# A new order for all engines' steps, and a fixed buffer for each batch

## The chip, the cores and the metric

The kernel runs on one core of a Trainium2 chip. The metric is the time of one execution on the device in microseconds; the runs of the kernel before took 207.67, 208.43 and 208.44 us, with a median of 208.43. The profile is of one execution, whose span (first to last instruction) is 205.4 us.

## The reference

`x` is 8 batches x 8 heads x 512 tokens x 64, `state` is 8 x 8 x 32 x 64. Attention goes both ways between tokens and states, and the joined rows (512 + 32 per batch, 8 heads x 64 = 512 wide, 4352 rows in all) go through a two-layer network with a PReLU:

```python
scores = x @ state^T / 8;  a = softmax(scores);   xread = a @ state
scores2 = state @ x^T / 8; a2 = softmax(scores2); sread = a2 @ x
rows = concat([xread, sread], axis=2)        # 544 rows of 512 per batch
h = rows @ w_in                              # 512 -> 2048
g = max(h, 0) + alpha * min(h, 0)
out = g @ w_out                              # 2048 -> 512, float32
```

## The kernel before

The whole program is one list of short tokens, `ORDER`. Each token names a step, with its batch, piece, PSUM bank and engine; a loop at the end of the kernel (line 830) calls the steps in this order. An engine runs its instructions in the order in which the tokens issue them, and a step starts when its inputs are there and the PSUM bank or buffer that it writes is free. There are eight PSUM banks, named in the tokens. So the order sets everything: which engine works on what, what queues behind a wait, and when transfers start.

The steps that matter here:

- Loads, all issued from GpSimd's queue: `lx0.g` (half the heads of batch 0, line 218), `lx.b` (x of a batch, line 201), `lst` (the states of batches 2 to 7, line 247), `wi.f` (a quarter of w_in, 512 of its columns, line 253), `wo.i` (a quarter of w_out, 512 of its rows, line 259). Stores `st.b.q` and halves `sv.b.q.h` go out on SP's queue, and so do the transposes by DMA, `xd` (line 327) and `tt` (line 541).
- States: `stt`, `sto`, `str`, `sro` transpose the states into `stT` (the copies out of PSUM: lines 300 and 317).
- Softmax for tokens: `sc` (scores on TensorE, line 362), `sb` (VectorE transposes them in blocks of 32), `smax`, `ssh` (GpSimd, line 482), `sexp` (ScalarE), `ssum`, `snorm` (GpSimd, line 496), `wb` (transposed back: the weights `aT`). Batch 0 goes by `sd`, `hm`, `hs`, `he` instead. Softmax for states: `tm`, `tms`, `te` (ScalarE, line 527), `tt`, `rd`, `rn`, `rt`, `rdo`.
- First layer without xread: since xread = a @ state, xread @ w_in is a @ (state @ w_in). `m.b.f` forms the product of a batch's states with a quarter of w_in (line 590, eight small matmuls side by side in two banks), `mo` copies its two halves out of PSUM (line 603, ScalarE or VectorE). `F.b.jc` (two matmuls, line 620; `f` is one of the two, line 641) gives one of 16 blocks of hidden rows from the weights and these products. For the state rows (b = 8) `F` goes the plain way with four matmuls (line 629). `N` is ScalarE's negative part (line 652), `G` VectorE's combination of both (line 656).
- Second layer: batch 0 in plain form, `S.b.q.i` (two matmuls of 512 columns, line 675) and `O`. All others by Strassen's scheme, with seven products instead of eight: `W` (sums of the blocks of w_out, GpSimd, line 745), `A.b.i.s.f` (sums of hidden rows, GpSimd or VectorE, line 765), `P.b.i.p.half` (four matmuls of 256 columns, line 793), `C` (copies out, line 805), `D` (added on, line 810). The products of one output lie in one bank one after the other, with a copy between: `P..1`, `C..1`, `P..6`, `C..2`, `P..7`, `C..3`, `P..4`, `C..4`.
- `Z.k.n` runs matmuls over zeros, n units of 128 columns.

Buffers that each batch needs anew (`xg`, `xT`, `ts`, `mx`, `r1`, `an`, `aT`, `e2`, `e2T`, `sn`) come from a pool that gives them out in turn, two to four of a kind. Sums of hidden rows have two buffers of a kind and half (the last number of an `A` token), output rows four.

Of the kernel before, what the change touches and what calls it, by code (L numbers as in the profile page):

```python
# [34 lines left out]
G.1.4 F.1.8.7 N.1.8.1 G.1.8 S.0.1.5 S.0.2.5 N.1.1.2 G.1.1 F.1.2.4 N.1.2.3 G.1.2 F.1.15.1 N.1.15.0
G.1.15 S.0.1.6 S.0.1.7 O.0.1.a.0 F.1.10.3 N.1.10.1 G.1.10 S.0.2.6 S.0.0.4 xd.2 sc.2.2.6.7 sb.2 tm.2
m.4.2.2.4 mo.4.2.a.0.12 smax.2 S.0.2.7 O.0.2.a.1 mo.4.2.a.1 S.0.3.0.1 F.1.9.3 N.1.9.2 G.1.9 tsum.1
F.1.11.2 N.1.11.3 G.1.11 W.0.0.p W.2.1.p W.0.1.p W.2.0.p W.3.1.p W.3.0.p A.1.0.3.0.p.0 A.1.1.3.0.p.1
tms.2 te.2.1 F.1.6.5 N.1.6.0 G.1.6 S.0.3.1 S.0.3.2 F.1.7.4 S.0.0.5 te.2.0 N.1.7.1 G.1.7 S.0.0.6
S.0.0.7 O.0.0.a.2 tt.0 tt.1 rd.0.3 rd.1.6 rn.1 A.1.1.1.0.v.0 A.1.0.3.1.v.0 m.2.3.7.2 mo.2.3.a.0.13  # L40
mo.2.3.a.1 xd.3 st.0.2 st.0.1 tt.2 S.0.3.3 F.1.13.5 ssh.p.2 sexp.2 N.1.13.2 m.3.1.0.4 mo.3.1.a.1.1
mo.3.1.a.0 A.1.1.2.0.p.0 rn.0 sc.3.2.6.7 tm.3 tms.3 lx.4 A.1.0.1.0.p.1 ssum.2 snorm.p.2 S.0.3.4
P.1.1.1.0.2 F.1.14.3 P.1.1.1.1 G.1.13 N.1.14.3 G.1.14 A.1.1.1.1.p.0 S.0.3.5 S.0.3.6 P.1.0.2.0.4
P.1.0.1.0.0 S.0.3.7 te.3.0 te.3.1 tt.3 sb.3 P.1.1.2.0.5 P.1.1.2.1 C.1.1.1.a.3 D.1.1.0 P.1.0.1.1
O.0.3.a.1 st.0.3 st.0.0 tsum.2 wb.2 m.2.2.3.1 mo.2.2.a.1.4 mo.2.2.a.0 m.3.2.6.7 mo.3.2.a.0.6 rd.2.5
lx.5 xd.4 A.1.1.2.1.p.0 P.1.0.2.1 mo.3.2.a.1 rt.0.1 rdo.0.a rn.2 smax.3 P.1.1.6.0 A.1.0.2.0.v.1
A.1.0.4.0.p.0 F.2.7.3 N.2.7.0 G.2.7 F.2.1.5 N.2.1.1 G.2.1 C.1.0.1.a.0 D.1.0.0 F.2.8.6 N.2.8.2 G.2.8
F.2.2.7 F.2.3.1 N.2.2.3 N.2.3.0 G.2.2 P.1.0.6.0 F.2.5.3 N.2.5.1 P.1.1.6.1 F.2.0.5 N.2.0.2 G.2.5
G.2.3 P.1.0.5.0.4 C.1.1.2.a F.2.11.6 N.2.11.3 G.2.11 G.2.0 A.1.0.1.1.p.1 P.1.0.5.1 F.2.9.7 P.1.1.7.0
F.2.10.3 N.2.10.1 xd.5 G.2.10 F.2.4.1 N.2.9.0 G.2.9 F.2.14.6 N.2.4.3 G.2.4 N.2.14.2 G.2.14  # L50
A.1.1.3.1.p.1 A.1.0.2.1.p.1 P.1.0.6.1 C.1.0.2.a P.1.1.7.1 ssh.p.3 sexp.3 ssum.3 P.1.1.5.0.5 F.2.13.3
rt.2.7 rdo.2.a P.1.0.7.0 C.1.1.3.a.1 P.1.0.7.1 C.1.0.3.a.2 D.1.0.1 F.2.12.1 N.2.12.1 F.2.6.6
P.1.1.5.1 G.2.12 N.2.6.0 F.2.15.7 N.2.15.3 A.1.0.4.1.p.0 G.2.6 G.2.15 N.2.13.2 G.2.13 P.1.0.4.0
P.1.0.4.1 A.2.0.1.0.p.1 C.1.0.4.a A.1.1.4.0.p.1 P.1.0.3.0 A.2.1.3.0.p.1 P.1.0.3.1 D.1.0.2 st.1.0
D.1.1.1 P.1.1.4.0 P.1.1.4.1 C.1.1.4.a st.1.3 tsum.3 rd.3.6 rn.3 sc.4.2.0.1 snorm.p.3 wb.3 m.3.3.7.3
m.4.1.4.2 mo.4.1.a.0.9 mo.3.3.a.1.0 mo.3.3.a.0 A.1.1.4.1.p.1 A.2.0.2.0.p.1 P.1.1.3.0 mo.4.1.a.1
A.2.1.1.0.v.0 A.2.0.4.0.v.0 P.2.0.1.0.6 P.2.0.1.1 P.2.0.2.0.4 C.2.0.1.a.0 F.3.5.3 N.3.5.1
A.2.0.1.1.v.1 A.2.0.2.1.p.1 F.3.1.7 N.3.1.0 tm.4 tms.4 P.2.0.6.0 P.2.0.2.1 D.2.0.0 G.3.5 F.3.3.2
# [804 lines left out]
```

## Time and profile before

| | |
|---|---|
| median of the runs | 208.43 us (207.67 to 208.44) |
| span of the profiled execution | 205.4 us; its time around the span isn't listed, the median is 3.03 us above the span |
| busy | TensorE 197.1 us (96%), VectorE 181.6 (88%), GpSimd 159.6 (78%), ScalarE 145.2 (71%) |
| granted TensorE clock | 1.00 by the profile, in all stretches |
| first S (second layer of batch 0) | starts at 25.12 us |
| TensorE's last matmul | ends at about 201.9 us |
| HBM | 17.31 MB read, 8.91 MB written |

Busy time is the union of an engine's instructions, and a matmul's end is modelled, so a busy TensorE need not run at its pace. In the views, a row of the timeline gives the start, the length, the engine, the line, the operation, and in brackets the idle time before it with what ended it; x4 means that four like instructions are merged in one row.

### The profile page before, as it was taken

The numbers are of one execution on the slowest core, as the hardware profiler recorded it, in microseconds if no ns is written. First come the engines' busy times: TensorE is split into PE (matmuls) and PEld (weight loads), VectorE is DVE, ScalarE is ACT, GpSimd is POOL, SyncE is SP. The second block draws the span as 40 slices with busy tenths as digits, with TensorE's granted clock in tenths as the row PEclk, the third lists the DMA queues.
The fourth block names the chain that finished last, engine by engine and source line by source line (L and its number), as shares of the span: only waits on it lengthen the run. The fifth ranks groups of instructions, "written<-read, shape, count | busy, mean of one in ns | idle before, by whom it ended". The sixth has DMA issues, their size and how long they took to land.

```text
span 205.4 us, 5181 instructions
## 1 busy us (share of the span) xinstructions
PE 197.1 (96%) x2023; PEld 131.4 (64%) x2023; DVE 181.6 (88%) x321; ACT 145.2 (71%) x319; POOL 159.6 (78%) x136
## 2 busy tenths in 40 slices
PE   7887999999999999999999999999999999999993
PEld 2542344445757766766557776776778777788882
DVE  4799999999999989999899999989999699995841
ACT  2599997889897679899898878869666476411120
POOL 7575489999989979998998899987997988502220
PEclk9999999999999999999999999999999999999999
DMA  5999999995999342749990135022000220031124
GB/s 81 195 203 209 204 206 197 185 232 54 163 163 178 66 153 58 100 103 158 194 163 3 53 123 135 3 105 102 0 0 3 111 93 3 2 131 62 69 102 156
DMA packets 39257, 23.22 MB, mean 113 GB/s; under 512 B 22320, under 2 KB 35008, under 8 KB 39232
## 3 DMA queue, kind: packets, MB, share of 16 engines
q0 software_dynamic: 12704, 8.59, 29.3%
q1 hardware_dynamic: 26496, 14.29, 28.4%
q8 instruction: 16, 0.26, 0.6%
q14 instruction: 9, 0.07, 0.2%
q10 hardware_dynamic: 32, 0.01, 0.0%
HBM read 17.31 MB, written 8.91 MB: 128 GB/s over the span
## 4 chain that ended last, share of the span: by engine, by line
PE 85%; DVE 5%; DMA 5%; POOL 1%; ACT 1%; issue 1%; ACTq 0%; POOLq 0%
PE ps L793 44%; PE ps L620 24%; PE ps L675 7%; DMA xg<-in_x_dram 5%; PE ps L629 3%; PE ps L590 3%; DVE gt_all L656 3%; PE ps L553 1%; ACT neg_all L652 1%; PE ps L362 1%; DVE m_all L603 1%; POOL xg L218 1%; DVE ts L466 1%; DVE nb L514 1%; DVE mx L476 1%
## 5 line engine op out<-in xcount | busy, mean ns | idle before, releaser
L656 DVE SCALAR_TENSOR_TENSOR gt_all<-neg_all,oma_sb,ps 128x512 f16<-128x512 f32 x128 | 89.3, 738 | 3.0 <-ACT neg_all L652 2.7
L652 ACT ACTIVATE neg_all<-ps 128x512 f32<-128x512 f32 (+1 forms) x144 | 77.4, 598 | 20.0 <-PE ps L620 14.4
L620 PE MATMUL ps<-aT,m_all 128*128 128x512 f16 x250 | 66.4, 379 | 0.3 <-DVE m_all L603 0.2
L765 POOL TENSOR_TENSOR hc_all<-gt_all 128x512 f16<-128x512 f16 x43 | 49.2, 1160 | 11.4 <-DVE osb_all L810 8.7
L793 PEld LDWEIGHTS <-hc_all 128*128 128x128 f16 x480 | 46.3, 98 | 14.3 <-issue 1.1
L793 PE MATMUL ps<-wc,hc_all 128*128 128x256 f16 x360 | 47.7, 273 | 0.0
L793 PEld LDWEIGHTS <-gt_all 128*128 128x128 f16 x336 | 32.6, 98 | 8.3 <-issue 0.5
L805 ACT COPY osb_all<-ps 128x256 f32<-128x256 f32 x51 | 19.1, 383 | 25.7 <-PE ps L793 22.2
L620 PEld LDWEIGHTS <-m_all 128*128 128x128 f16 x250 | 24.0, 98 | 18.0 <-issue 2.2
L603 ACT CAST m_all<-ps 128x512 f16<-128x512 f32 x58 | 31.6, 621 | 4.3 <-PE ps L590 4.3
L765 POOL TENSOR_TENSOR hc_all<-gt_all,hc_all 128x512 f16<-128x512 f16 x22 | 25.4, 1164 | 6.3 <-DVE hc_all L765 6.1
L793 PE MATMUL ps<-w_out_sb,gt_all 128*128 128x256 f16 x224 | 29.7, 273 | 0.0
L765 POOL TENSOR_TENSOR hc_all<-hc_all,gt_all 128x512 f16<-128x512 f16 x21 | 24.3, 1164 | 3.9 <-DVE hc_all L765 3.6
L810 DVE TENSOR_TENSOR osb_all<-osb_all,ps 128x256 f32<-128x256 f32 x45 | 18.0, 413 | 7.6 <-PE ps L793 4.7
L496 POOL TENSOR_TENSOR an<-ts,r 128x1024 f16<-128x1024 f32 (+1 forms) x9 | 15.5, 1725 | 6.2 <-DVE r L493 4.0
L482 POOL TENSOR_TENSOR ts<-ts,mx 128x1024 f32<-128x1024 f32 x7 | 13.4, 1918 | 5.4 <-DVE mx L476 5.4
L675 PE MATMUL ps<-w_out_sb,gt_all 128*128 128x512 f16 x64 | 16.6, 380 | 0.1
L793 PE MATMUL ps<-w_out_sb,hc_all 128*128 128x256 f16 x120 | 16.5, 273 | 0.0
L793 PE MATMUL ps<-wc,gt_all 128*128 128x256 f16 x112 | 14.7, 273 | 0.0
L590 PE MATMUL ps<-w_in_sb,stT 64*32 64x512 f16 x256 | 11.8, 383 | 1.9 <-DMA w_in_sb<-in_moe_w_in_dram 0.9
L527 ACT ACTIVATE e<-ps,nb 128x512 f16<-128x512 f32 x16 | 11.1, 705 | 0.1
L675 PEld LDWEIGHTS <-gt_all 128*128 128x128 f16 x64 | 5.9, 98 | 7.2 <-issue 1.2
(78 smaller groups left out, 204.6 us busy)
## 6 DMA issues: line engine op xcount, KB each, us to landing
out_dram<-osb_all SPq DMA_DIRECT2D x33, 256.0 KB, 2.6
xg<-in_x_dram POOLq DMA_DIRECT2D x7, 512.0 KB, 9.1
w_in_sb<-in_moe_w_in_dram POOLq DMA_DIRECT2D x4, 512.0 KB, 12.0
w_out_sb<-in_moe_w_out_dram POOLq DMA_DIRECT2D x4, 512.0 KB, 13.6
xg<-in_x_dram POOLq DMA_DIRECT2D x2, 256.0 KB, 4.5
out_dram<-osb_all SPq DMA_DIRECT2D x2, 128.0 KB, 2.4
gs_all<-in_state_dram POOLq DMA_DIRECT2D x1, 192.0 KB, 6.8
st<-in_state_dram SPq DMA_DIRECT2D x1, 128.0 KB, 2.4
```

The source lines that it names most:

```text
L482: engine(e).tensor_tensor(ts, ts, over_blocks(cols(softmax_tile("mx", b), j, S // N)), ALU.subtract)
L496: engine(e).tensor_tensor(blocks(cols(softmax_tile("an", b), j, S)), blocks(cols(softmax_tile("ts", b), j, S)), over_blocks(cols(softmax_t ...
L590: nc.tensor.matmul(banks[N * k : N * (k + 1), (k0, k1)[g], :], st_head(b, 2 * k + g)[64 * g : 64 * g + 64, :], w_in_sb[64 * g : 64 * g + 6 ...
L603: copier(e)(ms[b, f][:, g, :], banks[:, live["mp", b, f][g], :])
L620: nc.tensor.matmul(h.rearrange("p (r t) -> p r t", r=2), ms[b, f][:, g, 128 * j : 128 * (j + 1)], weights(b, g), start=(g == 0), stop=(g = ...
L652: nc.scalar.activation(neg, h, RELU, bias=0.0, scale=-1.0)
L656: nc.vector.scalar_tensor_tensor(gts[b, f][:, j, :], negs.pop((b, jc)), oma_sb[:, jc : jc + 1], hs.pop((b, jc)), ALU.mult, ALU.add,)
L675: nc.tensor.matmul(outs[b, q], hidden(b, jc, q), w_out_sb[:, jc, :], start=(jc == 0), stop=(jc == n_jc - 1),)
L765: engine(e).tensor_tensor(t, x, y, ALU.add if s == 1 else ALU.subtract)
L793: nc.tensor.matmul(outs[b, i, bank], rows, cols, start=(p in (1, 2, 5) and jc == 0), stop=(jc == n_jc // 2 - 1), skip_group_check=True,)
L805: copier(e)(rows_at(b, q, k)[:, 256 * half : 256 * (half + 1)], outs[b, i, "x"])
L810: nc.vector.tensor_tensor(to, to, outs[b, i, bank], ALU.add)
```

## The change: a new order, and homes

All tokens of `ORDER` stand in a new order, with other PSUM banks. The steps of the sum stay (210 P, 144 F with their N and G, 32 S, 120 A, 64 mo, all loads and stores). What differs in kind: zero matmuls 66 units instead of 73, in other places; 96 hidden sums on GpSimd and 24 on VectorE instead of 88 and 32; 59 `mo` copies on ScalarE and 5 on VectorE instead of 58 and 6; both copies of the later states (`sro`) on ScalarE instead of one on each engine; one `xo` more on ScalarE, and one `dd` less.

The start of the order, before and after:

```diff
-lx0.0 lx0.1 id ni.v wi.0 oma lst stc Z.7.32 stt.2 sto.a lx.1 wi.1 dd.0.0.v wi.2 Z.7.3 xt.0.0.0.6
...
-xo.0.0.1.a sd.0.1.6 hm.0.1 sc.0.2.1.2 tm.0 hs.0.0 he.0.0 ssum.0.0 wi.3 Z.3.2 hs.0.1 he.0.1 ssum.0.1
-m.1.0.7.4 mo.1.0.a.1.0 m.0.0.3.0 mo.0.0.a.1.1 tms.0 mo.0.0.a.0 str.0.5 sro.0.a str.1.6 sro.1.v
-mo.1.0.v.0 snorm.p.0.0 wb.0.0 snorm.p.0.1 wb.0.1 wo.0 wo.1 wo.2 te.0.1 te.0.0 Z.4.17 m.2.0.0.3
-mo.2.0.a.1.2 mo.2.0.a.0 Z.4.5 xt.1.1.0.5 xt.1.0.0.5 xo2.1.0.v xt.1.1.1.6 xt.1.0.1.6 xo2.1.1.v
...
+lx0.1 lx0.0 lst id wi.0 ni.v stc Z.7.32 stt.0 dd.0.0.v Z.7.7 xt.0.1.1.1 xt.0.0.1.2 dd.0.1.v xo.0.1.1.v oma
+xo.0.0.1.a lx.1 sto.a Z.7.11 xt.0.1.0.3 xt.0.0.0.4 xo.0.0.0.a xo.0.1.0.v sd.0.1.5 hm.0.1 str.1.6 sd.0.0.7
+sc.0.2.1.2 sro.1.a hm.0.0 hs.0.1 he.0.1 tm.0 Z.0.3 hs.0.0 he.0.0 ssum.0.1 ssum.0.0 str.0.0 sro.0.a Z.3.12
+m.0.0.3.4 m.4.0.6.5 m.2.0.7.0 wi.1 mo.0.0.v.1.0 tms.0 wo.0 wi.2 wo.1 te.0.0 te.0.1 wi.3 mo.0.0.a.0 m.1.0.1.2
+mo.2.0.a.0.1 snorm.p.0.1 m.3.0.4.3 snorm.p.0.0 wo.2 lx.2 wb.0.1 mo.4.0.v.0.2 wb.0.0 mo.1.0.a.0.3 xt.1.1.0.7
+xt.1.0.0.7 xo2.1.0.v mo.3.0.a.1.4 xt.1.1.1.6 xt.1.0.1.6 mo.1.0.v.1 xo2.1.1.v f.0.0.0.1 f.0.0.1 wo.3
+f.0.2.0.3 mo.3.0.a.0 mo.2.0.a.1 mo.4.0.a.1 N.0.0.0 F.0.3.4 f.0.1.0.7 f.0.1.1 N.0.3.1 G.0.0 m.0.1.0.5 N.0.1.2
...
```

The first S steps, and the end of the order:

```diff
-S.0.1.0.2 S.0.1.1 S.0.2.0.5 S.0.2.1 m.2.1.6.4 mo.2.1.v.0.10 sexp.1 ssum.1 snorm.p.1 N.0.6.1 G.0.6
...
-P.7.0.5.1 D.7.0.0 D.7.0.1 A.7.0.4.1.v.1 P.7.0.4.0 P.7.0.4.1 C.7.0.4.a st.7.1 P.7.1.7.0 P.7.1.7.1
-C.7.1.3.a.3 P.7.1.5.1 D.7.1.1 sv.7.3.1 P.7.0.3.0 P.7.0.3.1 D.7.0.2 st.7.0 A.7.1.4.0.p.0 P.7.1.3.0
-P.7.1.3.1 D.7.1.2 st.7.2 P.7.1.4.0 P.7.1.4.1 C.7.1.4.a sv.7.3.0
+m.2.1.0.5 mo.2.1.a.0.7 mo.2.1.a.1 tms.1 mo.1.1.a.1 te.1.0 F.0.4.7 F.0.6.6 F.0.5.0 N.0.5.0 G.0.2 te.1.1
+S.0.3.0.5 S.0.3.1 S.0.1.0.3 S.0.2.0.4 N.0.4.1 sb.1 smax.1 lx.3 W.1.0.p ssh.p.1 S.0.1.1 m.0.2.1.2 G.0.5 G.0.4
...
+P.7.0.4.0 C.7.1.2.a P.7.1.7.0 P.7.1.7.1 C.7.1.3.a.0 P.7.0.4.1 P.7.0.3.0 P.7.0.3.1 D.7.1.1 D.7.0.2 st.7.0
+sv.7.3.1 C.7.0.4.a st.7.1 P.7.1.3.0 P.7.1.3.1 D.7.1.2 P.7.1.4.0 P.7.1.4.1 C.7.1.4.a st.7.2 sv.7.3.0
```

The buffers are no longer given out in turn. Each kind has its buffers by number, as many as before, and a table says which one a batch uses:

```diff
+HOMES = {
+    "xg": "01230231",
+    "xT": "01010101",
...
+    "mx": "00101010",
...
+    "e2": "01202102",
+    "e2T": "00110101",
+    "sn": "00110110",
+}
...
+    homes = {
+        kind: [consts.tile(shape, dtype, name=f"{kind}_{i}") for i in range(n)]
+        for kind, (n, shape, dtype) in kinds.items()
+    }
+
+    def home(kind, b):
+        return homes[kind][int(HOMES[kind][b])]
...
     def load_x(b):
-        xg = xgs[b] = att.tile([128, H, 2, 2, D], F16, name=f"xg_{b}", tag="xg", bufs=4)
+        xg = xgs[b] = home("xg", b)
```

Two further edits leave no trace in the work: the pool `att` now only holds small tiles, with eight buffers, and the loop reads `ORDER` alone.

More of the change, by code (lines that the diff above doesn't have):

```diff
@@ L35 @@
[L35 to L58, printed above, removed]
@@ L214 @@
     nc.scalar.dma_start(al32[:n_jc, :], moe_alpha.rearrange("(jc p) -> jc p", p=128))
-    xgs[0] = att.tile([128, H, 2, 2, D], F16, name="xg_0", tag="xg", bufs=4)
+    xgs[0] = home("xg", 0)
     def load_x0(g):
@@ L322, in x_tile @@
         if ("xT", b) not in live:
-            live["xT", b] = att.tile([128, H, 2, 128], F16, name=f"xT_{b}", tag="xT", bufs=2)
+            live["xT", b] = home("xT", b)
         return live["xT", b]
@@ L452, in softmax_tile @@
         if (kind, b) not in live:
[L453 to L460 removed]
+            live[kind, b] = home(kind, b)
         return live[kind, b]
@@ L522, in token_exp @@
         if ("e2", b) not in live:
-            live["e2", b] = att.tile(
-                [128, 2, n_q, 128], F16, name=f"e2_{b}", tag="e2", bufs=3
-            )
+            live["e2", b] = home("e2", b)
             live["r2", b] = att.tile([128, 2], F32, name=f"r2_{b}", tag="r2", bufs=8)
@@ L539, in token_transposed @@
     def token_transposed(b):
-        e2T = live["e2T", b] = att.tile([128, 2, n_q, 128], F16, name=f"e2T_{b}", tag="e2T", bufs=2)
+        e2T = live["e2T", b] = home("e2T", b)
         nc.sync.dma_start_transpose(
@@ L563, in state_reads_norm @@
     def state_reads_norm(b):
-        sn = live["sn", b] = att.tile([128, 2, D], F16, name=f"sn_{b}", tag="sn", bufs=2)
+        sn = live["sn", b] = home("sn", b)
         nc.vector.tensor_tensor(
@@ L829 @@
     }
-    for token in (globals().get("TOKENS") or ORDER).split():
+    for token in ORDER.split():
         name, *args = token.split(".")
```

210 lines of the change are left out of this document (115 added, 95 removed).

## The prediction

> **What bounds the kernel now.** I read the page first (span, chain), then the busy time by stretch, then the chain in order of time, then single rows.
>
> ```profile
> span 205.4 us, 5181 instructions
> ...
> PE 85%; DVE 5%; DMA 5%; POOL 1%; ACT 1%; issue 1%; ACTq 0%; POOLq 0%
> ```
>
> The chain is TensorE for 85%. The span is 205.4; the median of the runs is 208.43, so 3.03 lie around the span, and I add them unchanged. The sum is made in the span.
>
> ```profile
> 10.00:15.00 5.00, 3.96 (x67) 2.16 (x67) 4.68 (x9) 4.74 (x12) 3.56 (x5) 1.00 1.35 202
> 15.00:20.00 5.00, 4.21 (x65) 1.54 (x63) 4.78 (x6) 4.40 (x11) 3.24 (x4) 1.00 1.24 206
> 20.00:25.00 5.00, 4.29 (x36) 1.55 (x36) 5.00 (x9) 5.00 (x13) 1.76 (x1) 1.00 1.24 207
> 30.00:40.00 10.00, 10.00 (x48) 4.54 (x47) 10.00 (x15) 7.97 (x16) 9.94 (x5) 1.00 1.28 192
> 40.00:60.00 20.00, 20.00 (x269) 10.89 (x267) 19.72 (x32) 17.70 (x41) 18.87 (x15) 1.00 0.89 157
> 60.00:80.00 20.00, 20.00 (x206) 14.12 (x204) 19.18 (x33) 15.62 (x35) 18.50 (x16) 1.00 0.62 126
> 202.00:203.00 1.00, 0.00 (x0) 0.00 (x0) 0.00 (x0) 0.29 (x1) 0.00 (x0) 1.00 1.00 371
> 203.00:204.00 1.00, 0.00 (x0) 0.00 (x0) 0.00 (x0) 0.00 (x0) 0.00 (x0) 1.00 0.46 154
> ```
>
> Columns: stretch, length, busy time of PE, PEld, DVE, ACT, POOL, then clock, DMA share, GB/s. From 10 to 25 us ScalarE and VectorE are nearly full and the loads run at 202 to 207 GB/s; from 30 us TensorE is full, VectorE nearly so (19.72 and 19.18 of 20). Busy PE is not PE at its pace, so I count steps:
>
> ```profile
> 25.12 1.46 PE ps L675 x6
> ```
> ```profile
> 34.19 2.16 PE ps L620 x10
> ```
> ```profile
> 41.87 0.22 PE ps L590 x8
> 42.09 0.97 PE ps L675 x4
> 43.06 0.65 PE ps L620 x3
> ```
> ```profile
> 184.96 16.93 PE ps L793 x155
> ```
>
> A first-layer step F is two matmuls of the 34.19 row (0.43); a second-layer step S the same; a product step P is four matmuls of the last row (0.44); a state product m is 0.22. Leaving a group of small-tile steps costs 0.11 (0.97 for four matmuls instead of 0.86), and entering one I take as the same. From the first S at 25.12 to the end of TensorE at 184.96 + 16.93 = 201.89 lie 176.8 us. The steps in the order behind that point are 32 S, 118 F of batches, 16 of the state rows at 0.44, 210 P, 22 m (172.6 with the small ones), and some 16 groups of small-tile steps (3.5): 176.1. So nothing is lost after 25 us. A new order can gain only ahead of that, in the number of groups, and in the tail; it can lose anywhere.
>
> **The change part by part.** *Loads.* The queue of loads on GpSimd was x0, x0, w_in 0, states, x1, w_in 1 to 3, w_out 0 to 3, x2, x3; it becomes x0, x0, states, w_in 0, x1, w_in 1, w_out 0, w_in 2, w_out 1, w_in 3, w_out 2, x2, w_out 3, x3.
>
> ```profile
> 10.13 0.62 PE L590 MATMUL ps<-w_in_sb,stT 64*32 64x512 f16 x16 [0.43 <-DMA w_in_sb<-in_moe_w_in_dram]
> 11.08 0.86 PE L286 MATMUL ps<-ident,gs_all 128*64 128x128 f16 x24 [0.32 <-DMA gs_all<-in_state_dram]
> 11.87 1.09 PE L272 MATMUL ps<-gs_all 128*128 128x512 f16 x5
> 13.09 0.41 PE L590 MATMUL ps<-w_in_sb,stT 64*32 64x512 f16 x8
> 13.43 0.45 PE L272 MATMUL ps<-gs_all 128*128 128x512 f16 x2
> 14.34 0.45 PE L340 MATMUL ps<-ident,xg 128*128 128x128 f16 x5 [0.47 <-DMA xg<-in_x_dram]
> ```
>
> States and w_in 0 swap: 0.19 MB at about 205 GB/s is 0.95 us, so the states come at about 8 and w_in 0 at 11.1; x1 stays at 14.3, w_in 1 follows one 0.52 MB piece (2.5 us) later at 16.9 as before. Then w_out 0 at 19.4, w_in 2 at 21.9 (2.5 later), w_out 1 at 24.5, w_in 3 at 27 (5 later), w_out 2 at 29.5, w_out 3 at 34.6 (2.5 later). The two w_out issues that now stand ahead of the normalisation on GpSimd fall in its wait for VectorE: nothing.
>
> *The first stage.* With states early, the products of w_in 0 for batches 0, 4, 2, 1, 3 stand together, and S steps of batch 0 can start with half of w_out. But the first stage is ScalarE's, in order: every product m needs two copies out of PSUM, every F a negative. Its paces:
>
> ```profile
> 12.13 0.83 ACT L317 COPY stT<-ps 128x768 f16<-128x768 f16 x1
> 12.83 0.72 ACT L527 ACTIVATE e<-ps,nb 128x512 f16<-128x512 f32 x1
> 13.41 0.23 ACT L527 ACTIVATION_READ_ACCUMULATOR e<-ps,nb 128x1 f32 x1
> 13.50 0.72 ACT L527 ACTIVATE e<-ps,nb 128x512 f16<-128x512 f32 x1
> ```
> ```profile
> 21.64 2.10 ACT L603 CAST m_all<-ps 128x512 f16<-128x512 f32 x4
> ...
> 23.54 2.65 ACT L652 ACTIVATE neg_all<-ps 128x512 f32<-128x512 f32 x5
> ```
>
> State copy 0.70 start to start, token exponential 0.67, copy 0.52, negative 0.53. In the new order one state copy moves from VectorE to ScalarE, ahead of the score exponentials, which then start about 9.6. Behind: two exponentials (1.2), the other state copy (0.7), two token shifts (0.2), four token exponentials (2.7), one state exponential (1.0), 20 copies (10.4), 15 negatives (7.9): 24.1, so ScalarE reaches the negative of F.0.15 at 33.6 if it never waits, and TensorE, which follows it bank by bank, stands at 33.45 with 16 F, 12 m and 14 S done. Before, the same 16 F and 12 m with 13 S were done at 34.19 (its row above is the next step). Lead: 0.74 + 0.43 = 1.2 us. ScalarE was idle 0.6 us of 15 to 20, so waits of its own may take 1 us of the lead; if negatives come out better than that, by the S that need no ScalarE, it is up to 2.2. I take 1.2.
>
> *Zero matmuls.* Two fillers of 17 and 5 units that stood at 11.87 and 13.43 go; others move.
>
> ```profile
> 1.32 3.17 PE L272 MATMUL ps<-gs_all 128*128 128x512 f16 x7 [1.32 <-DVE gs_all L266]
> ```
>
> The first seven take 0.45 each, the five at 11.87 0.22 each: TensorE starts at half pace and is later at full. The Trainium skill (TensorE: Matmul & The Clock Gate, part 1) says that an idle window of about 3.4 us halves the clock again; the trace shows the start of that, no relapse. Without a relapse the fillers are worth nothing; with one, see the third rival.
>
> *Small-tile groups.* Counted in the order behind the checkpoint: 15 against 14, at 0.22: +0.2.
>
> *GpSimd.* 96 hidden sums instead of 88 (VectorE loses eight).
>
> ```profile
> 25.12 4.21 POOL L745 TENSOR_TENSOR wc<-w_out_sb 128x1024 f16<-128x1024 f16 x2
> ```
> ```profile
> L765 POOL TENSOR_TENSOR hc_all<-hc_all,gt_all 128x512 f16<-128x512 f16 x21 | 24.3, 1164 | 3.9 <-DVE hc_all L765 3.6
> L496 POOL TENSOR_TENSOR an<-ts,r 128x1024 f16<-128x1024 f32 x7 | 13.4, 1918 | 2.7 <-ACT osb_all L805 1.5 <-ACT neg_all L652 0.7 <-DVE r L493 0.5
> L482 POOL TENSOR_TENSOR ts<-ts,mx 128x1024 f32<-128x1024 f32 x7 | 13.4, 1918 | 5.4 <-DVE mx L476 5.4
> ```
> ```profile
> 50.18 0.94 POOL L201 DMA_DIRECT2D xg<-in_x_dram  x1
> ```
>
> After the normalisation of batch 1 (30.25 by the steps above) come, to the sum A.2.0.2.0: six weight sums at 2.11 (12.7), two shifts and two normalisations at 1.9 (7.6), two load issues (1.8), 25 hidden sums at 1.14 start to start (28.5): 80.9. TensorE needs it for P.2.0.6.0: from 33.45, 42 F, 39 P, 18 S, 7 m and small steps, 48.4 with 7 groups: 81.9. One us of room, where by the same count the tightest place before had 2.6. In 40 to 80 us GpSimd was idle 1.13 + 1.50 = 2.6; if it is so again, 1.6 are late. Much of that idle time was GpSimd running ahead of its inputs, so I take 0.4, with ends 0 and 1.6. VectorE, eight sums lighter, has no less room than now: nothing, and what covers it is ScalarE and GpSimd being late first.
>
> *Homes.* One buffer per batch by a table instead of rotation changes which release a load or write waits for, and no instruction. Loads of x4 to x7 stand behind the reads of the batch that held their buffer: nothing. On SP's queue the x transposes of 4 and 5 follow their loads by 3.1 and 1.4 us of TensorE work and hold up stores behind them; score steps use them 6 and 7 us later: nothing if they land, and in the stall term otherwise.
>
> *Tail.*
>
> ```profile
> 199.80 0.34 SPq L726 DMA_DIRECT2D out_dram<-osb_all  x1
> 200.62 1.20 SPq L722 DMA_DIRECT2D out_dram<-osb_all  x2
> 202.31 0.33 SPq L726 DMA_DIRECT2D out_dram<-osb_all  x1
> ```
>
> Four stores stand at the end (half, whole, whole, half of 256 KB). In the new order st.7.1, another whole one, goes out between them, because its last product P.7.0.4 is now next to last but five. At 371 GB/s (202 to 203) 0.26 MB take 0.7 us, and the queue was full then, so the last half lands later: +0.8 with its issue; ends 0 and 1.1.
>
> Sum: 205.4 - 1.2 + 0.2 + 0.4 + 0.8 = 205.6; with 3.03 around, 208.6.
>
> **The rivals.** *Faster:* the half of w_out pays more than the ScalarE sum says, since S steps need neither of the two full engines. For it: 4.29 of 5 busy in 20 to 25 is mostly waiting and S could fill it from 21. Against: batch 0's S wait for its hidden rows, 15 negatives deep in ScalarE. With 2.2 lead, no stall, 0.3 of tail: 205.4 - 2.2 + 0.2 + 0.3 = 203.7, so 206.7. *Slower:* GpSimd becomes the bound at batch 2, P.2.0.6 waiting for its hidden sum; it decides once GpSimd idles over 1.0 us between 30 and 81, and with 2.6 idle there and the same again at batch 3, 3.2 late, no 0.4: 208.4, so 211.4. Against: its inputs, counted the same way on VectorE, are ready in time by a few tenths. *Cold clock:* from 9.9 to 14.3 TensorE has only some 2.5 us of work where the fillers stood. If the pace halves, the four transposes of x1 (1.0), four F (1.7) and an m by 18 us take 3.0 more, 0.6 of it hidden by ScalarE: 211.0. By the Trainium skill's window (same page and part) that needs 3.4 us without work; the longest gap I count is 1.3.
> *No effect:* what comes earlier isn't what bounds: lead 0, and the rest as summed, 206.8 and with 3.03 around 209.8, just past the forecast's own range.
>
> **How the numbers follow.** About 0.5% is what a measurement of this kernel can tell from no change: 207.4 to 209.5. Forecast, same: 0.40. Faster rival 0.30; GpSimd 0.18, clock 0.05, no lead 0.07, all slower: 0.30. The forecast's own range is 207.4 to 209.5; both signs hold much, so the range reaches from lead 2.2 without stall or tail, 206.4, to the GpSimd case, 211.4.
>
> **What would show it.** Right: first L675 row near 21 to 22; the wait for the states gone; ScalarE's x15 negatives done near 33.6; F.1.9 near 33.5; P rows of batch 2 without GpSimd as releaser; TensorE's end near 201.3, and 4.3 us from there to the end of the span instead of 3.5. Wrong: ScalarE idle between 10 and 33, hc_all from POOL among TensorE's releasers between 50 and 110, or L620 pairs above 0.43 near 15 us.

## The result, and the profile after

The changed kernel takes 231.68 us (median of 4 runs, 231.29 to 231.86), the kernel before beside it 208.16 (207.67 to 208.44): a ratio of 1.112, 95% interval 1.108 to 1.116. The forecast was 208.6, in a range of 206.4 to 211.4. The profiled execution has a span of 229.5 us, 24.1 more than before, and took 231.29. In three of the kernels below (g2_moved, g3_transpose_later, k1_load_later) one run of four was more than 1.5% longer than the fastest, and their times are medians of the other three.

The page of the changed kernel: span, busy time, the granted clock in 40 slices, the chain by engine, and VectorE's sums of hidden rows that read two blocks of gt_all.

```profile
span 229.5 us, 5165 instructions
...
PE 205.0 (89%) x2020; PEld 132.8 (58%) x2020; DVE 194.1 (85%) x311; ACT 148.6 (65%) x321; POOL 169.8 (74%) x144
...
PEclk9999889999997699999999999999999999999998
...
PE 39%; DVE 10%; ACT 3%; issue 3%; ACTq 0%
...
L779 DVE TENSOR_TENSOR hc_all<-gt_all 128x512 f16<-128x512 f16 x18 | 22.4, 1247 | 0.2
```

The like row of before, from the full list of groups by line:

```profile
L765 DVE TENSOR_TENSOR hc_all<-gt_all 128x512 f16<-128x512 f16 x13 | 5.4, 426 | 0.0
```

The chain that the page follows goes back only to 98.5 us here, and TensorE carries 39 of the 55% of the span that it covers; before it was 85 of 98%. VectorE has eight sums fewer and is busy 12.5 us longer: a sum of the row shown takes 1247 ns in the mean, before 426, and all 24 together take 25.9 us, where the 32 before took 13.6. TensorE's waits and the rows behind the longest one, in the timelines of TensorE, VectorE and GpSimd:

```profile
24.74 0.41 PE L604 MATMUL ps<-w_in_sb,stT 64*32 64x512 f16 x8 [1.36 <-DVE ts L482]
26.65 0.73 PE L634 MATMUL ps<-aT,m_all 128*128 128x512 f16 x2 [0.96 <-DVE gt_all L670]
72.71 1.01 PE L634 MATMUL ps<-aT,m_all 128*128 128x512 f16 x2 [6.41 <-DVE gt_all L670]
```
```profile
23.43 1.25 DVE L482 STREAM_TRANSPOSE ts<-ps 128x1024 f32<-128x1024 f32 x1 [2.26 <-ACT e L541]
...
63.88 1.21 DVE L492 TENSOR_REDUCE mx<-ts 128x32 f32<-128x1024 f32 x1
65.01 6.99 DVE L779 TENSOR_TENSOR hc_all<-gt_all 128x512 f16<-128x512 f16 x1
71.92 3.37 DVE L670 SCALAR_TENSOR_TENSOR gt_all<-neg_all,oma_sb,ps 128x512 f16<-128x512 f32 x5
```
```profile
63.31 0.94 POOL L224 DMA_DIRECT2D xg<-in_x_dram  x1
64.26 2.27 POOL L779 TENSOR_TENSOR hc_all<-gt_all,hc_all 128x512 f16<-128x512 f16 x2
66.49 1.14 POOL L779 TENSOR_TENSOR hc_all<-gt_all 128x512 f16<-128x512 f16 x1
67.60 1.90 POOL L498 TENSOR_TENSOR ts<-ts,mx 128x1024 f32<-128x1024 f32 x1
69.47 2.25 POOL L779 TENSOR_TENSOR hc_all<-gt_all,hc_all 128x512 f16<-128x512 f16 x2
80.67 1.16 POOL L779 TENSOR_TENSOR hc_all<-gt_all 128x512 f16<-128x512 f16 x1 [8.96 <-DVE gt_all L670]
```

One VectorE sum, A.1.0.3.1, takes 6.99 us. It ends when six GpSimd instructions that stand back to back have ended (69.47 + 2.25 = 71.72). PReLU steps queue behind it, TensorE waits 6.41 us for them, and so does GpSimd, for 8.96. Near 23 us VectorE waits 2.26 us to transpose scores out of banks that ScalarE's token exponentials read, and TensorE waits twice behind that. Before, TensorE waited nowhere over 0.15 us after 22 us. By stretches, the clock is the third number from the end:

```profile
27.00:31.00 4.00, 4.00 (x19) 1.31 (x18) 3.64 (x6) 2.91 (x5) 3.19 (x3) 0.58 1.37 200
72.00:78.00 6.00, 5.29 (x17) 2.46 (x17) 4.79 (x7) 2.28 (x4) 0.00 (x0) 0.50 0.34 62
```

At both waits the granted clock fell to half, for about 3.4 us from 27.0 on and for 6.8 from 71.3.

### The profile page after: what moved, and what is told of

Same layout as the page of the kernel before. It is cut to its first block, busy times and chain, and to the rows that moved or that the text cites. A ratio compares the mean times of both kernels' runs of the same rounds, so it can differ in the third digit from the quotient of the medians.

```text
span 229.5 us, 5165 instructions
## 1 busy us (share of the span) xinstructions
PE 205.0 (89%) x2020; PEld 132.8 (58%) x2020; DVE 194.1 (85%) x311; ACT 148.6 (65%) x321; POOL 169.8 (74%) x144
## 4 chain that ended last, share of the span: by engine, by line
PE 39%; DVE 10%; ACT 3%; issue 3%; ACTq 0%
PE ps L807 26%; PE ps L634 9%; DVE gt_all L670 4%; DVE hc_all L779 3%; PE ps L643 2%; ACT e L541 2%; PE ps L604 1%; ACT neg_all L666 1%; DVE osb_all L824 1%; PE ps L567 1%; DVE nb L530 0%; DVE aT L520 0%; DVE gs_all L670 0%; DVE osb_all L819 0%; ACT osb_all L819 0%
## 5 line engine op out<-in xcount | busy, mean ns | idle before, releaser
L666 ACT ACTIVATE neg_all<-ps 128x512 f32<-128x512 f32 (+1 forms) x144 | 78.2, 585 | 35.4 <-PE ps L634 19.3
L634 PE MATMUL ps<-aT,m_all 128*128 128x512 f16 x250 | 69.8, 390 | 11.1 <-DVE gt_all L670 9.4
L779 POOL TENSOR_TENSOR hc_all<-gt_all 128x512 f16<-128x512 f16 x38 | 43.7, 1163 | 19.8 <-DVE gt_all L670 13.1
L807 PE MATMUL ps<-wc,hc_all 128*128 128x256 f16 x360 | 48.3, 276 | 2.1 <-ACT osb_all L819 2.1
L807 PEld LDWEIGHTS <-gt_all 128*128 128x128 f16 x336 | 32.5, 98 | 10.0 <-issue 1.8
L779 POOL TENSOR_TENSOR hc_all<-gt_all,hc_all 128x512 f16<-128x512 f16 x28 | 32.3, 1167 | 4.2 <-DVE hc_all L779 4.1
L779 POOL TENSOR_TENSOR hc_all<-hc_all,gt_all 128x512 f16<-128x512 f16 x23 | 26.8, 1173 | 3.1 <-DVE hc_all L779 2.5
L779 DVE TENSOR_TENSOR hc_all<-gt_all 128x512 f16<-128x512 f16 x18 | 22.4, 1247 | 0.2
L498 POOL TENSOR_TENSOR ts<-ts,mx 128x1024 f32<-128x1024 f32 x7 | 13.6, 1938 | 11.0 <-DVE mx L492 11.0
L689 PE MATMUL ps<-w_out_sb,gt_all 128*128 128x512 f16 x64 | 17.3, 395 | 0.0
L807 PE MATMUL ps<-wc,gt_all 128*128 128x256 f16 x112 | 15.6, 273 | 0.0
```

The lines of the kernel that those rows point to most:

```text
L634: nc.tensor.matmul(h.rearrange("p (r t) -> p r t", r=2), ms[b, f][:, g, 128 * j : 128 * (j + 1)], weights(b, g), start=(g == 0), stop=(g = ...
L666: nc.scalar.activation(neg, h, RELU, bias=0.0, scale=-1.0)
L689: nc.tensor.matmul(outs[b, q], hidden(b, jc, q), w_out_sb[:, jc, :], start=(jc == 0), stop=(jc == n_jc - 1),)
L779: engine(e).tensor_tensor(t, x, y, ALU.add if s == 1 else ALU.subtract)
L807: nc.tensor.matmul(outs[b, i, bank], rows, cols, start=(p in (1, 2, 5) and jc == 0), stop=(jc == n_jc // 2 - 1), skip_group_check=True,)
```

## The experiments

Two theories stood at the start: that VectorE's sums and GpSimd's work shut each other out (L), and that the new order simply asks for results too early, or of a too full engine (B). The short names are those of the tokens; `.p` is GpSimd, `.v` VectorE. In each kernel only what the diff shows differs.

**Two sums on GpSimd** (e1_two_sums).

```diff
-A.1.1.2.0.v.1   -A.1.0.3.1.v.0
+A.1.1.2.0.p.1   +A.1.0.3.1.p.0
```

> The changed kernel with two of VectorE's hidden sums, A.1.1.2.0 and A.1.0.3.1, given to GpSimd; nothing else moves. In the changed kernel's profile they are VectorE's sums at 59.75 us (1.37 us) and at 65.01 us (6.99 us, over GpSimd instructions that stand back to back). Theory L (a sum on VectorE and an instruction on GpSimd shut each other out, and VectorE loses its turn as long as GpSimd has no pause): the 6.99 goes, with it TensorE's idle 6.41 us at 72.71 and most of the slow pace behind it; GpSimd gets 2.3 us more; 8 to 10 us less, so 222 to 224. Theory B (the new order asks for results later than they can be made, whoever makes them): GpSimd is fuller by two sums, 231.7 to 234.

Measured: 223.28 us (222.54 to 223.85), 8.4 less, as theory L has it. But VectorE also has less work here, so the exclusion isn't shown by this alone.

**All 24 sums on GpSimd** (e2_all_sums).

> The changed kernel with all 24 hidden sums that VectorE has given to GpSimd (120 there), nothing else moved. Theory L: the 15.8 us that VectorE's sums take above 0.42 each are gone, but GpSimd has 24 x 1.14 = 27 us more work, where it was busy 169.8 of 229.5: 216 to 221 if GpSimd's free time takes it up. Theory B: GpSimd is later for 24 x 1.14, 236 to 245.

Measured: 231.16 us (229.80 to 231.73), in neither range. Behind the place of the long sum TensorE is 6 to 9 us ahead of the changed kernel up to about 190 us, and loses nearly all of it at the end, where GpSimd is late. TensorE's waits of that kernel begin with

```profile
PE ps L816 <- POOL hc_all L788: 9.7, 11, 2.1
```

**Homes alone** (e3_homes). The order of before in the form of the changed kernel, `"xg": "01230123"`, `"e2": "01201201"`, `"e2T": "01011001"`, `"sn": "10010110"`. With this last table batches 2 and 4 overwrite a small buffer of batch 1 before it is read, so batch 1's state rows hold other numbers; the instructions are the same.

> The order of the kernel before, in the changed kernel's form with one named buffer per batch; the table repeats the old rotation. Homes alone, with the choice of buffers as before. Theories L and B: 207.7 to 208.7, the time before. Theory H (buffers named once for the whole program wait otherwise than buffers given out in turn): 215 or more.

Measured: 208.01 us beside 207.84, ratio 1.003 (1.000 to 1.006). Named buffers cost nothing that can be told. The table of the changed kernel was not run alone.

**Block transpositions first** (e4_blocks_first).

```diff
-te.1.0 ... sb.1     -te.2.1 te.2.0 ... sb.2     -te.7.0 ... te.7.1 rt.5.3 sb.7
+sb.1 te.1.0 ...     +sb.2 te.2.1 te.2.0 ...     +sb.7 te.7.0 ... te.7.1 rt.5.3
```

> The changed kernel with three steps moved, as the kernel before has them: VectorE's transposition of the scores (sb.1, sb.2, sb.7) ahead of ScalarE's token exponentials of the same batch (te.1.0, te.2.1, te.7.0), which read the same PSUM banks. If VectorE's wait for ScalarE's reads is a cause by itself: the idle 1.36 and 0.96 us of TensorE near 25 us and the half pace behind them (1.7 us) go, and some of 1.02 + 0.41 + 0.46 near 140 us: 2.5 to 4 less, 227.5 to 229. If ScalarE's later exponentials cost as much elsewhere: 231 to 232.

Measured: 228.29 us (227.32 to 228.98), 3.4 less. TensorE's rows of this kernel:

```profile
32.88 2.75 PE L643 MATMUL ps<-aT,m_all 128*128 128x512 f16 x12
...
41.72 0.41 PE L394 MATMUL ps<-xT,stT 64*32 64x256 f16 x16 [2.20 <-DMA xT<-xg]
```

The first row is six F steps, the third of them F.1.9: 32.88 + 2 x 0.43 = 33.75. The prediction put TensorE at 33.45 there. So the early lead is real; in the changed kernel F.1.9 comes at 36.9. And a new wait appears at 41.7, for x of batch 2. There and at half pace behind it (clock 0.50 from 44 to 46 us) most of the lead is lost again. Of the rest of the gain 0.9 us isn't the start's: the long sum takes 6.12 us here, and TensorE waits 5.54 for it instead of 6.41.

**A bench for the exclusion** (f1_bench), appended to the kernel before:

```diff
+    nc.vector.tensor_copy(zs, ...)            # GpSimd's sums wait for this
+    nc.vector.scalar_tensor_tensor(...)       # reads PSUM
+    for i in range(n): nc.gpsimd.tensor_tensor(m_all[:, 2 + i, 0, :], zs, gt[:, 8 + i, :], ALU.subtract)
+    for i in range(3): <one kind of VectorE instruction>
```

> The kernel before with a bench appended behind its last step, which writes nothing that the output reads. In each round VectorE writes a buffer that 6 GpSimd sums (128x512 f16, two operands in SBUF, 1.14 us each) wait for, does one PSUM-reading PReLU step, and then three instructions of one kind; each kind also runs once with GpSimd at rest, and the sum also beside 1, 2 and 3 GpSimd sums. Theory L: the first sum with two f16 operands in SBUF waits until the GpSimd sums that stand back to back are done: about 1, 2, 3 us beside 1, 2, 3, and 5 to 6.5 beside six; at rest 0.35 to 0.42; the PReLU step, the sum onto an output row and the copy out of PSUM (one operand or none in SBUF) take the same beside GpSimd as at rest. Rival T (the engines take turns, each waits at most for one instruction of the other): each of the three sums 1.1 to 1.4 beside six. Rival B (no exclusion, what made the sum of 6.99 us long was its data): 0.42 everywhere. Nobody has numbers for the copy within SBUF, the block transposition and the reduction.

VectorE's rows of the sum at rest, the sum beside six, and the PReLU step beside six:

```profile
204.90 1.09 DVE L847 TENSOR_TENSOR m_all<-gt_all 128x512 f16<-128x512 f16 x3
...
206.76 3.51 DVE L847 TENSOR_TENSOR m_all<-gt_all 128x512 f16<-128x512 f16 x3
...
228.59 2.06 DVE L851 SCALAR_TENSOR_TENSOR m_all<-neg_all,oma_sb,ps 128x512 f16<-128x512 f32 x3
```

Three sums take 1.09 us at rest, 1.61, 2.55 and 3.51 beside one, two and three GpSimd sums, and 3.51 beside six. Each waits for one GpSimd instruction and then gets its turn: rival T, and not L as I had put it. A three-operand step with both large operands in SBUF goes from 2.07 to 4.38, a copy within SBUF from 0.69 to 3.18. The PReLU step (2.06 and 2.06), the sum onto an output row (1.32), the copy out of PSUM (1.88), the block transposition (3.49) and the reduction (3.72) take the same in both. The Trainium skill (SBUF — State Buffer, Who interferes with whom) has this list: a VectorE instruction with two SBUF inputs, or a copy in a mode that takes two ports, shares a port pair with GpSimd, and the one that comes second is blocked for the whole instruction of the other; one with at most one SBUF input otherwise, or a reduction, never is. The trace agrees. It leaves the 6.99 us unexplained: six turns lost.

**A dose of VectorE sums in the order of before** (f2_dose).

```diff
-A.1.0.2.1.p.1  A.1.1.3.1.p.1  A.2.0.1.0.p.1  A.2.1.3.0.p.1
+A.1.0.2.1.v.1  A.1.1.3.1.v.1  A.2.0.1.0.v.1  A.2.1.3.0.v.1
```

> The kernel before, its own order, with four hidden sums in GpSimd's dense stretch given to VectorE (A.1.0.2.1, A.1.1.3.1, A.2.0.1.0, A.2.1.3.0): four sums fewer on GpSimd (4.6 us), four more on VectorE (1.7 us at 0.42). Theory L: they stand beside GpSimd work that is back to back, take 1.3 to 6 us each, 8 to 16 us together, and most of it passes to TensorE, since VectorE has only 1.1 us of 40 free there: 213 to 222. Theory B: only 1.7 us more on VectorE and 4.6 less on GpSimd: 206.5 to 209.5.

Measured: 213.11 us (212.56 to 213.72). The time lies at the edge of L's range, but for another reason: no sum is long (381 to 526 ns). GpSimd, whose next sums build on these, waits for VectorE, and TensorE waits 3.3 us in turn and then runs at half pace (clock 0.50 from 67.5 to 70.9 us):

```profile
POOL hc_all L765 <- DVE hc_all L765: 17.5, 8, 5.2
```

So this run does not speak for the exclusion. It shows that VectorE, in order and full, is the wrong place for a sum that GpSimd waits for.

**One token two steps earlier** (f4_one_step_earlier).

```diff
-A.1.1.2.1.p.1 P.1.1.5.0.0 G.2.2 smax.3 A.1.0.3.1.v.0
+A.1.1.2.1.p.1 P.1.1.5.0.0 A.1.0.3.1.v.0 G.2.2 smax.3
```

> The changed kernel with one token moved: VectorE's sum A.1.0.3.1 two VectorE steps earlier, ahead of a PReLU step and a reduction, so that it meets the 0.94 us at 63.31 in which GpSimd issues a load, not the six GpSimd instructions behind it. No engine gets more or less work. Theory L: its 6.99 us become 0.4 to 1.3 and the 6.41 us wait goes: 222.5 to 225. Theory B (VectorE or GpSimd has too much to do around 65 us): 230.5 to 232.

Measured: 221.85 us (221.49 to 222.68), 9.8 less, with every engine's work unchanged. VectorE's row of the sum and GpSimd's load issue beside it:

```profile
63.07 0.41 DVE L788 TENSOR_TENSOR hc_all<-gt_all 128x512 f16<-128x512 f16 x1
```
```profile
63.13 0.94 POOL L233 DMA_DIRECT2D xg<-in_x_dram  x1
```

6.99 became 0.41. It isn't VectorE's load but the neighbour: theory B falls for this wait. The first TensorE step behind the wait comes 6.7 us earlier (65.97 for 72.71), and the transposition of the state rows behind it 9.4 (70.77 for 80.15), since the half pace that followed the wait is gone too.

**Both edits.** First the two sums on GpSimd with the transpositions (f3_both), then the moved sum with the transpositions (g2_moved).

> The changed kernel with both edits that helped alone: the two hidden sums on GpSimd (8.4 us less alone) and the three block transpositions ahead of the token exponentials (3.4 less alone). If they are two causes at two places: 219.5 to 221. If the second only moved the start of the first wait, or GpSimd becomes late: 222 to 224.

> The changed kernel with the sum A.1.0.3.1 two VectorE steps earlier (9.8 us less alone) and the three block transpositions ahead of the token exponentials (3.4 less alone); no work changes its engine. If both causes are apart: 218 to 219. If the edit at the start shifts the sum off the pause that it was moved into: 224 to 229.

Measured: 220.63 us and 219.59. The first is as expected, the second 0.6 over. Alone the transpositions brought 3.4, beside the moved sum 2.3; 0.9 of the first figure came from the long sum, as said. The clock at the start doesn't explain the difference: the kernel with the moved sum has 1.00 from 27 to 31 us, where the changed kernel has 0.58, but then waits 1.32 us near 42 us for x of batch 2, and both reach the same step at 51.27 and 51.44 us.

**What made one sum lose six turns** (g1_bench2). A second bench: one VectorE sum beside one GpSimd sum, (a load issue,) and six sums; with or without a reduction right ahead of it.

> A second bench behind the last step of the kernel before, again without effect on the output: one VectorE sum at a time beside a GpSimd row of one sum, (a load issue,) and six sums. In the first bench each sum beside six waited for one GpSimd instruction at most (three took 3.5 us together); in the changed kernel one waited through six. The rounds differ in what stood around that one: whether GpSimd issued a load ahead of the row, whether VectorE did a reduction right before the sum or a PSUM-reading step, whether a subtraction on 128x1024 float32 stands in the row, and at which phase the sum comes (five rounds with 1 to 5 reciprocals ahead). Theory R (the reduction before the sum), theory Q (the load issue, behind which GpSimd's next instructions stand ready), theory W (the wide instruction): the rounds with it show one sum of 3 to 7 us, the others 0.4 to 1.4. If it was the moment at which it came: one or two of the thirteen are long, without a common mark.

VectorE's sums, in this order: no load, after a reduction; load; load, a wide instruction in the row; load, after a reduction. Below, GpSimd's rows of the first and second:

```profile
222.55 1.36 DVE L875 TENSOR_TENSOR m_all<-gt_all 128x512 f16<-128x512 f16 x1
...
242.17 5.39 DVE L875 TENSOR_TENSOR m_all<-gt_all 128x512 f16<-128x512 f16 x1
...
252.13 6.13 DVE L875 TENSOR_TENSOR m_all<-gt_all 128x512 f16<-128x512 f16 x1
...
262.39 5.81 DVE L875 TENSOR_TENSOR m_all<-gt_all 128x512 f16<-128x512 f16 x1
```
```profile
220.14 8.10 POOL L850 TENSOR_TENSOR m_all<-m_all,gt_all 128x512 f16<-128x512 f16 x7 [0.41 <-DVE m_all L857]
...
239.64 0.94 POOL L860 DMA_DIRECT2D m_all<-in_x_dram  x1
240.60 6.68 POOL L850 TENSOR_TENSOR m_all<-m_all,gt_all 128x512 f16<-128x512 f16 x6
```

All three sums in a row behind a load issue wait until the row ends (240.60 + 6.68 = 247.28; the sum ends at 247.56). The three without one take 0.93, 0.93 and 1.36. Neither the reduction nor the wide instruction matters: theory Q. It isn't the transfer itself that keeps VectorE out, since it ended well before the sum did (the last number is GB/s):

```profile
244.00:245.00 1.00, 0.00 (x0) 0.00 (x0) 1.00 (x1) 0.00 (x0) 1.00 (x1) 0.50 0.91 122
245.00:246.00 1.00, 0.00 (x0) 0.00 (x0) 1.00 (x1) 0.00 (x0) 1.00 (x2) 0.50 0.01 1
246.00:247.00 1.00, 0.00 (x0) 0.00 (x0) 1.00 (x1) 0.00 (x0) 1.00 (x2) 0.50 0.00 0
```

In the other seven rounds the reduction shared a buffer with the wide instruction, so the sum came when the row was nearly over; they say nothing.

**The load alone, in the changed kernel** (k1_load_later).

```diff
-lx.4 ... A.1.1.4.0.p.0 ... A.1.1.4.1.p.0 A.1.1.3.1.p.1 ... ssh.p.3
+A.1.1.4.0.p.0 ... A.1.1.4.1.p.0 A.1.1.3.1.p.1 ... lx.4 ssh.p.3
```

> The changed kernel with one token moved: the load of x of batch 4 on GpSimd's queue from ahead of three hidden sums to behind them (ahead of the subtraction of batch 3), 2.4 us later. The VectorE sum A.1.0.3.1 (6.99 us, then TensorE's wait of 6.41) stays where it is, beside the same GpSimd sums. Theory Q (behind a load issue GpSimd's back-to-back instructions keep VectorE's sum out until GpSimd pauses; without one VectorE gets its turn after one instruction): the sum takes 0.4 to 1.4 us, 221.5 to 224. If the load has nothing to do with it: the sum still takes 6 to 7, 230.5 to 232.

VectorE's sum and GpSimd's rows beside it:

```profile
65.23 0.86 DVE L788 TENSOR_TENSOR hc_all<-gt_all 128x512 f16<-128x512 f16 x1
```
```profile
63.55 2.26 POOL L788 TENSOR_TENSOR hc_all<-gt_all,hc_all 128x512 f16<-128x512 f16 x2
65.77 1.33 POOL L788 TENSOR_TENSOR hc_all<-gt_all 128x512 f16<-128x512 f16 x1
67.05 0.94 POOL L233 DMA_DIRECT2D xg<-in_x_dram  x1
```

The sum stands at the same place beside the same three GpSimd sums, and takes 0.86 us instead of 6.99. That settles theory Q in the kernel itself. The time, 225.29 us (225.14 to 227.11), is 1.3 over the range: x of batch 4 comes later, and TensorE waits 1.53 us for its transposition.

**What is left: x of batch 2.** The transposition by DMA of x of batch 3 later on SP's queue (`xd.3` behind `tt.0`, g3_transpose_later), then also its load later (`lx.3` ahead of `W.2.1.p`, k2_x3_later).

> The kernel g2_moved with one more token moved: the transposition by DMA of x of batch 3 behind the transposition of the exponentials of batch 0 on SP's queue, as the kernel before has it, instead of right behind that of batch 2. In the profile of the two edits together TensorE waits 1.56 us near 41 us for x of batch 2, whose transposition is issued at 32.4 and lands at about 41. If the two transpositions hold each other up: that wait goes, 1 to 1.6 us less than g2_moved. If the loads behind it are what makes it slow: the same as g2_moved within 0.5.

> The kernel g3_transpose_later with the load of x of batch 3 on GpSimd's queue behind the weight sum that follows the normalisation of batch 1's weights and three others (about 35 us), no longer in the first row of loads. TensorE waited 2.35 us near 41 us for the transposition of x of batch 2, issued at 32.4, while the last quarter of w_out and x of batch 3 were being loaded. If loads in flight are what makes the transposition slow: it lands 2 us earlier and the wait goes, 1.5 to 2.3 us less than g3_transpose_later (219.6), so 217.3 to 218.1. If the transposition waits for its own x of batch 2 only: 219.2 to 220.

Measured: 219.57 and 218.50 us. Moving the transposition did nothing (TensorE waited 2.35 us, before this edit 1.76; 219.57 against 219.59). With the load later the wait is gone; the span of the profiled execution fell by 2.5 us (217.9 to 215.4), the median by only 1.1, which lies between the two ranges. So the loads in flight made the transposition slow, not the other transposition.

**Five more sums** (k3_five_sums). A.3.0.1.1, A.3.1.1.1, A.3.1.3.1, A.4.1.1.1 and A.4.1.3.0 from VectorE to GpSimd.

> The kernel k2_x3_later with five of VectorE's hidden sums of batches 3 and 4 on GpSimd (they take 0.71 to 1.37 us each between 100 and 130 us, one GpSimd instruction's turn more than at rest): 2.9 us of waiting and 2.1 of work less on VectorE, 5.7 us more on GpSimd, which was busy 18.8 and 16.1 of 20 there. If these turns cause TensorE's waits for VectorE near 106 and 130 us (1.25 + 0.27 + 0.73): 1.5 to 2.3 less than k2_x3_later. If GpSimd becomes late in place of it: the same or up to 2 more. If the waits come from the order of steps: the same within 0.5.

Measured: 218.62 us, the same, but by exchange. TensorE's waits for VectorE near 104 and 128 us (1.25, 0.27 and 0.73) are gone, and waits for GpSimd's sums stand in their place:

```profile
PE ps L816 <- POOL hc_all L788: 2.4, 3, 0.9
```

So VectorE's other sums do hold TensorE up there, and GpSimd has no room to take them.

**Three tokens behind copies** (k4_behind_copies).

```diff
-te.4.0 C.2.1.1.a.1 ... N.3.7.3     -te.5.1 ... C.2.0.2.a C.2.1.4.a     -tm.7 A.4.1.3.0.v.1 ... D.3.1.2
+C.2.1.1.a.1 ... N.3.7.3 te.4.0     +C.2.0.2.a C.2.1.4.a te.5.1         +D.3.1.2 tm.7 A.4.1.3.0.v.1
```

> The kernel k2_x3_later with three tokens moved within their engine's row: ScalarE's token exponentials te.4.0 and te.5.1 behind the copies of product sums that stood behind them (ScalarE was idle 1.08 and 1.58 us ahead of them while VectorE read the same banks), and VectorE's sum onto an output row D.3.1.2 ahead of a reduction and a hidden sum. TensorE's waits at these places were 0.78, 1.30 and 1.01 us. If they come from what stands ahead of the copies: these three go, with the 0.16 us that TensorE needs to fill again after each, 2.5 to 3.5 less than k2_x3_later (218.5), so 215 to 216. If the copies are late for the product's own sake: 218 to 219.

One of the places in the kernel without this edit (k2_x3_later): VectorE reads the scores, ScalarE sits idle 1.58 us, the copy goes behind the exponential, TensorE waits 1.30 for it.

```profile
85.43 1.24 DVE L491 STREAM_TRANSPOSE ts<-ps 128x1024 f32<-128x1024 f32 x1
```
```profile
86.75 0.69 ACT L550 ACTIVATE e<-ps,nb 128x512 f16<-128x512 f32 x1 [1.58 <-issue]
...
87.43 0.63 ACT L828 COPY osb_all<-ps 128x256 f32<-128x256 f32 x2
```
```profile
87.84 0.60 PE L816 MATMUL ps<-wc,hc_all 128*128 128x256 f16 x4 [1.30 <-ACT osb_all L828]
```

Measured: 217.68 us (216.44 to 218.24), 0.8 less than 218.50 (218.12 to 218.83), not 2.5, and hardly clear of the spread. The three waits are gone, and TensorE's rows of the kernel with the edit show what came in their place: the exponentials, now later, hold the banks that TensorE wants next.

```profile
88.20 1.03 PE L816 MATMUL ps<-w_out_sb,gt_all 128*128 128x256 f16 x8 [0.84 <-ACT e L550]
...
126.73 1.46 PE L643 MATMUL ps<-aT,m_all 128*128 128x512 f16 x6 [1.32 <-ACT e L550]
```

**The new start with the old rest** (h1_start_only). The changed order up to about 39 us with the transpositions first, then the remaining tokens in the order of before, ten PSUM banks renamed.

> The changed kernel's start with the repaired order of the block transpositions (all steps up to about 39 us, loads included), and behind it the rest of the kernel before, in the order of the kernel before; buffers by a table, PSUM banks renamed at ten tokens where the two meet. The prediction's lead by itself: with the transpositions ahead TensorE reached its checkpoint at 33.75, where I forecast 33.45 and the kernel before, with one step fewer, stood at 34.19, so 0.9 us ahead. If the order behind the start is what loses, as I think: 206.8 to 208, 0 to 0.6% under the kernel before. If the early start itself costs something later (loads, x of batch 2): 209 to 212.

Measured: 214.91 us (214.56 to 216.20), outside both ranges. The start's lead is there again (F.1.9 at 33.8 us), but from 39 to 53 us TensorE waits 5.3 us, mostly for PReLU steps and copies that themselves wait for TensorE. I read this as the seam's fault: the new start has used up the F steps that the old order keeps between S steps. That isn't shown, and the run does not separate start and rest.

## Why the prediction was wrong

Step by step, against the sum 205.4 - 1.2 + 0.2 + 0.4 + 0.8:

- *The lead, -1.2.* Right in kind: the first S starts at 21.05 us (forecast 21 to 22), and with the block transpositions first F.1.9 comes at 33.75 (forecast 33.45). In the changed kernel it comes at 36.9. I counted what ScalarE does in order and took it never to wait; I did not look at who else reads the banks that it reads. VectorE's transposition stood behind ScalarE's exponentials of the same scores and waited 2.26 us; in neither trace does one of the seven score transpositions overlap a token exponential. The Trainium skill (PSUM — Partial Sum Buffer, PSUM bank collisions raise a hardware error) says that two engines must not touch a bank at once, reads included, and that programs have to keep them apart. The waits fit that; no run here shows what an overlap would do.
- *VectorE, "eight sums lighter, has no less room than now: nothing".* This is the step that failed most: 9.8 us. I counted VectorE's instructions and not what stands beside them on GpSimd. Before, 27 of the 32 sums met a pause of GpSimd and five a quarter of a microsecond of its work (0.38 to 0.54 us each, and GpSimd's own waits name them); in the new order more than half of them fall beside its work, 0.41 to 1.37 us, and one, behind a load issue, takes 6.99. In the profiles TensorE gains 9.4 us there when the sum is moved, 6.7 of them the wait and the rest the half pace behind it. The rivals had GpSimd late, never VectorE blocked by it.
- *GpSimd, +0.4.* No GpSimd wait of weight shows in the changed kernel; with VectorE's sums given to it, it is late at once (9.7 us of TensorE's waits).
- *Homes, nothing.* Right for the old choice of buffers (ratio 1.003, to 1.006). But the loads and the transpositions, priced with them at nothing for batches 4 and 5, were missed for batch 2: 1.56 to 2.35 us of wait once the start was in order.
- *Zero matmuls.* The cold clock did come, yet not between 9.9 and 14.3 us where the rival had it (1.00 there), but at the new waits. The rival also asked too much, 3.4 us without work in one piece: at 27 us the clock fell with no idle stretch over 1.36 us (more on this at the end).
- *Tail, +0.8.* Right in kind: 4.7 us from TensorE's end to the end of the span (224.83 to 229.5), forecast 4.3, before 3.5.
- *Around the span, 3.03.* In the later runs of the kernel before it is 1.7 to 1.9, with spans of 204.9 to 207.4; so the profiled 205.4 was one of its shorter executions. The sum came to the right start, 208.43, all the same.
- *"Nothing is lost after 25 us."* True of the order before, and carried over to the new one without a look. In the last of the repaired kernels TensorE still waits 6.3 us after 22 us, in ten places of over 0.2 us, and each costs 0.16 us more than its idle time: in a row a matmul of 0.27 us starts every 0.11 us, and at a wait that overlap is lost.

The difference of the medians was 23.5 us. The sum moved: 9.8. The transpositions first: 2.3. The load of x of batch 3: 1.1 (219.59 to 218.50, its transposition included). Three tokens: 0.8, hardly clear of the spread. So 14.0 are placed by runs and 217.68 is left, 9.6 over the kernel before beside it (208.05). Of these, waits are 6.3, the overlap lost at them 1.6 and the tail 1.2, read from the profile and not tested one by one; some half a microsecond, and the lead of about 0.9 that should have come off, are not placed. No kernel of this study beats the one before.

## What to carry to other kernels

Moving a step changes its neighbours, not only its queue: for each VectorE instruction with two SBUF operands look at what GpSimd runs at that moment, and put it where GpSimd waits, never behind a load that GpSimd issues. For each PSUM bank list all its readers in order; a second reader on another engine is a wait, and what queues behind it is late too. A sum of counted steps holds only for an order whose waits have been walked through; for a wholly new order, the loss is in the places not walked. For the clock add up TensorE's idle time over some microseconds instead of looking for the longest gap.

## What the runs showed of the hardware that I had not expected

- A VectorE sum with two SBUF operands normally waits for one GpSimd instruction (0.9 to 1.4 us beside a row of 1.14 us sums), but behind a load issued from GpSimd's queue it waits until the row pauses: 5.39, 5.81 and 6.13 us in the bench, 6.99 and 6.12 in two kernels. Why the load issue does that is open; in the bench its transfer was over by 245.4 us, 2.2 us before the sum ended. Instructions with an operand in PSUM, reductions and block transpositions took the same time beside six GpSimd sums as at rest.
- The granted clock fell to half behind idle stretches of only 1.36 and 0.96 us in a span of 3.3. The same two stretches (1.38 and 0.96) in the kernel with the moved sum left it at 1.00. The Trainium skill (TensorE: Matmul & The Clock Gate, part 1) speaks of an idle window of about 3.4 us that runs freely. In these traces the clock changes only on a grid of 3.41 us, whose phase differs between executions (in the changed kernel at 26.96, 30.38, 71.34 and 78.16 us: 1, 12 and 2 steps). Windows of that grid, of the changed kernel, and the two that hold the stretches in the kernel with the moved sum (length, TensorE's busy time, clock third from the end):

```profile
23.55:26.96 3.41, 1.26 (x12) 0.42 (x11) 3.38 (x4) 1.43 (x3) 0.94 (x1) 1.00 1.24 207
26.96:30.37 3.41, 3.41 (x16) 1.01 (x15) 3.38 (x6) 2.56 (x4) 3.06 (x2) 0.50 1.37 199
```
```profile
21.93:25.35 3.42, 2.04 (x17) 0.81 (x16) 1.86 (x2) 2.07 (x7) 0.00 (x0) 1.00 1.24 206
25.35:28.76 3.41, 2.45 (x18) 0.87 (x17) 3.41 (x6) 2.37 (x4) 2.72 (x2) 1.00 1.27 204
```

In the first both stretches fall into one window, 2.15 us idle in all, and the next window runs at half pace. In the second they fall into two, 1.38 and 0.96 us idle, and nothing happens. Over all profiles of this case a window at full pace with 1.99 us or more without work was followed by half pace, and one with 1.93 or less was not; so whether two short waits cost a relapse is partly luck.
- A transposition by DMA issued at 32.4 us landed at about 41 while two loads were in flight beside it, and early enough for TensorE once one of them was moved behind it; the row of its issue took 5.03 us with that load ahead (g3_transpose_later) and 2.97 with it behind (k2_x3_later).
